# Decode attention, one core: last V slab and last wo stripe in three pieces each, and unused matmuls in the tensor engine's last waits

## Chip, cores, metric

One core of one Trainium2 chip. The metric is device time in microseconds (us) of that core, as the median of several executions. The profile is one execution; its span is about 2 us shorter than the time reported for the same execution.

## The reference

Two independent copies (A and B) of a one-token attention step. The output is A and B side by side.

```python
# B=2 batches, D=576, Hq=32 query heads, Hkv=16 key/value heads, Sk=16384, Dh=128
W = min(4096, max(256, Sk // 4))                   # 4096: only the last 4096 cache rows
q = (x @ wq)...                                    # 2 x 32 heads x 128
k, v = k_cache[:, :, Sk-W:, :], v_cache[...]       # each kv head serves two query heads
p = softmax(q @ k.T * Dh**-0.5)
o = p @ v
return o.reshape(B, 1, Hq*Dh) @ wo                 # wo: 4096 x 576
```

Everything is bf16. K and V windows of A and B are 134 MB, and each byte is used once. So this is a streaming problem.

## The kernel before

The work is cut into 32 slabs (16 kv heads of A, then 16 of B). A slab is 2 MB of K and 2 MB of V. V of a slab lies in SBUF as 64 columns j: each is a 128 x 128 tile with 128 cache rows (64 of either batch entry) on the partitions. Four slabs make a group, and a group needs a stripe of wo (8 rows per partition, 1152 KB). All loads go out on SyncE's queue in a fixed order through a ring of eight 2 MB slots. The last loads of the program are V of slab 31 and then the last stripe of wo. Both are already cut in two:

```python
v_cut = KR - 8          # 56 of 64 columns, then 8
w_cut = 7               # 7 of 8 rows, then 1
...
# issue(), wo stripe i (last one: NG - 1)
cuts = [(0, 8, wo_sem[sl])] if i < NG - 1 else [(0, w_cut, wo_sem[sl]), (w_cut, 8, wlast_sem)]
...
# issue(), last V slab: two DMAs fa (columns 0..v_cut) and fb (v_cut..KR), each with its semaphore
```

What follows the last V columns is a chain over four engines:

```python
# make_PV, last group: V columns are the weights, 16 columns of p^T move
for j in range(j0, j1):
    # ...  (col is worked out from j)
    e.matmul(OL[m % 2][:, 0:16], ring[:, r, j*128:(j+1)*128], pT[:, v, col:col+16],
             start=(j == 0), stop=(j == KR - 1))
# make_A_last (VectorE): oA = OL * cmr            - normalise and spread
# make_rl     (TensorE): 2 matmuls with jmask     - bring the heads into the layout of wo
#             (ScalarE): oP = copy of the PSUM
# make_proj   (TensorE): for each of the 8 rows j of wo, two halves of 288 output columns
for j in range(j0, j1):
    for half in range(2):
        e.matmul(PJ[half], oP[:, v, j, :], wob[:, v, j, half*NH:(half+1)*NH], ...)
# PJ[0] and PJ[1] lie on different 32-partition groups of one PSUM bank.
# make_E: VectorE copies half 0, ScalarE half 1, then SyncE issues the output store.
```

## Time and profile before

| | before |
|---|---|
| time, median of 3 | 370.21 us (370.14 to 370.30) |
| span of the profile | 368.2 us |
| DMA | 153.1 MB at 416 GB/s over the span |
| TensorE busy | 72% |
| last wo landing that TensorE waited for | 363.43 us |
| from the start of the output copies to the end of the span | 2.56 us |

From the page of the kernel before. The second to fourth lines are slices of the span, forty to a row: granted TensorE clock in tenths, DMA busy in tenths, and GB/s. The last is the share of the chain of waits by engine.

```profile
span 368.2 us, 3673 instructions
...
PEclk9966998898998779658996988895898889788755
DMA  8999999999999999999999999999999999999992
GB/s 321 448 409 431 432 427 423 433 424 425 429 424 431 429 427 421 433 431 428 424 423 433 427 427 427 424 427 429 429 423 433 429 427 421 432 429 427 425 415 97
...
DMA 81%; DVE 12%; PE 5%; issue 1%; SPq 0%; ACT 0%
```

The DMA engines are full from the first slices to the last but one. So the kernel runs at the speed of its loads, and only what comes after the last bytes can be shortened without moving fewer bytes. PEclk ends in a 5: half clock (0.50 granted in every window from 353 to 365 us).

The end of the chain of waits (start, length, what):

```profile
330.02 33.41 DMA wob<-in_B_wo_dram
363.43 0.14 issue
363.57 1.84 PE pj L670 x14
365.41 0.28 PE pj L660 x2
365.69 0.43 DVE out_sb L680
```

The timeline of the same end (start, length, engine, line, operation, operands; in brackets the idle time of the engine before it and what ended that; PE is TensorE, PEld its weight loads, DVE VectorE, ACT ScalarE, SPq the sequencer of SyncE):

```profile
360.41 1.88 PE L583 MATMUL st<-pT,ring 128*128 128x16 bf16 x64 [2.44 <-DMA ring<-in_B_v_cache_dram]
...
362.60 0.22 PE L638 MATMUL tb<-jmask,oA 128*128 128x8 bf16 x2 [0.32 <-DVE oA L618]
362.86 0.19 ACT L642 ACTIVATE oP<-tb 128x16 bf16<-128x16 f32 x1 [15.49 <-PE tb L638]
...
363.57 1.84 PE L670 MATMUL pj<-wob,oP 128*2 128x288 bf16 x14 [0.75 <-DMA wob<-in_B_wo_dram]
...
365.20 0.45 PE L660 MATMUL pj<-wob,oP 128*2 128x288 bf16 x2
...
365.72 0.40 ACT L681 ACTIVATE out_sb<-pj 2x288 bf16<-2x288 f32 x1 [2.67 <-PE pj L660]
366.59 0.32 SPq L684 DMA_DIRECT2D out_dram<-out_sb  x1
```

PV of slab 31 waits 2.44 us for V. The projection waits for wo until 363.57 and then has 14 matmuls ahead of it before it can take the last two. The store is issued 0.47 us after ScalarE's copy ended (365.72 + 0.40 = 366.12).

### The profile page before, as it was taken

The page shows a single profiled execution, that of the slowest core. Times are in us where ns is not written, and L with a number is a line of the kernel's source. Part 1 is how long each engine was busy: PE and PEld are TensorE (multiplying, and loading weights), DVE is VectorE, ACT ScalarE, POOL GpSimd, SP SyncE. Part 2 cuts the span into 40 slices and gives each one's busy share as a digit, 9 for nine tenths or more (in the row PEclk, how much of TensorE's full clock was granted, in tenths as well). Part 3 has the DMA queues.
Part 4 walks back from the last instruction along what each step waited for, and adds up shares of the span by engine and source line. Part 5 has one row for each costly group of instructions (what it writes and reads, how often), then busy time and mean ns, then how long its engine had stood idle before and what let it go on. Part 6 is the DMA issues. An engine that isn't in the chain of part 4 may idle for free.

```text
span 368.2 us, 3673 instructions
## 1 busy us (share of the span) xinstructions
PE 265.2 (72%) x1686; PEld 98.0 (27%) x1430; DVE 186.0 (51%) x189; ACT 34.3 (9%) x114; POOL 14.2 (4%) x53
## 2 busy tenths in 40 slices
PE   0635975897759499597869697777968678489754
PEld 0311111122114122242215221242313122144543
DVE  2105986967642774444843774436744476342000
ACT  1011002002000110002000110002000030003000
POOL 5010000000000000000000000000000000000000
PEclk9966998898998779658996988895898889788755
DMA  8999999999999999999999999999999999999992
GB/s 321 448 409 431 432 427 423 433 424 425 429 424 431 429 427 421 433 431 428 424 423 433 427 427 427 424 427 429 429 423 433 429 427 421 432 429 427 425 415 97
DMA packets 10976, 153.34 MB, mean 416 GB/s; under 512 B 1224, under 2 KB 1360, under 8 KB 1616
## 3 DMA queue, kind: packets, MB, share of 16 engines
q1 hardware_dynamic: 10948, 153.10, 98.0%
q8 instruction: 12, 0.20, 0.2%
q14 instruction: 4, 0.03, 0.0%
q10 hardware_dynamic: 12, 0.01, 0.0%
HBM read 153.10 MB, written 0.00 MB: 416 GB/s over the span
## 4 chain that ended last, share of the span: by engine, by line
DMA 81%; DVE 12%; PE 5%; issue 1%; SPq 0%; ACT 0%
DMA ring<-in_B_k_cache_dram 41%; DMA ring<-in_A_k_cache_dram 27%; DVE xt L426 11%; DMA wob<-in_B_wo_dram 9%; DMA ring<-in_A_wq_dram 4%; PE st L450 2%; PE st L381 1%; PE ot L274 1%; PE pj L670 1%; PE tb L607 0%; SPq L373 0%; DVE out_sb L680 0%; DVE ssum L525 0%; DVE nMrep L484 0%; PE pj L660 0%
## 5 line engine op out<-in xcount | busy, mean ns | idle before, releaser
L426 DVE STREAM_TRANSPOSE xt<-ring 128x2048 f32<-128x2048 f32 x64 | 144.4, 2287 | 88.8 <-DMA ring<-in_A_k_cache_dram 44.6
L450 PE MATMUL st<-xt,zq 128*128 128x512 bf16 x256 | 113.9, 445 | 63.6 <-DVE xt L426 63.3
L381 PE MATMUL st<-xt,zq 128*128 128x512 bf16 x256 | 114.5, 447 | 0.0
L450 PEld LDWEIGHTS st<-xt,zq 128*128 128x128 bf16 x256 | 28.0, 109 | 158.0 <-DVE xt L426 86.6
L574 PE MATMUL ot<-ring,pT 128*32 128x512 bf16 x448 | 58.7, 409 | 1.4 <-DMA ring<-in_B_v_cache_dram 0.7
L574 PEld LDWEIGHTS ot<-ring,pT 128*32 128x32 bf16 x448 | 21.4, 102 | 37.6 <-issue 18.9
L607 PEld LDWEIGHTS tb<-selv,oE 128*128 128x128 f32 x112 | 18.1, 245 | 5.7 <-issue 4.0
L413 POOL TENSOR_TENSOR zq<-qs,bmask 128x64 bf16<-128x64 bf16 x32 | 9.3, 294 | 270.0 <-PE st L381 189.9
L607 PE MATMUL tb<-selv,oE 128*128 128x16 f32 x112 | 17.0, 297 | 0.8 <-ACT oE L597 0.8
L626 DVE TENSOR_TENSOR oA<-tb,cmask 128x256 bf16<-128x256 f32 x7 | 3.0, 425 | 28.5 <-PE tb L607 28.5
L597 ACT ACTIVATE oE<-ot,rsb 128x512 f32<-128x512 f32 x14 | 9.6, 685 | 81.1 <-PE ot L574 81.1
L501 ACT ACTIVATE pR<-st,bias_sb 128x256 bf16<-128x256 f32 x32 | 15.9, 545 | 0.3
L583 PE MATMUL st<-pT,ring 128*128 128x16 bf16 x256 | 7.5, 174 | 5.8 <-DMA ring<-in_B_v_cache_dram 5.8
L670 PE MATMUL pj<-wob,oP 128*2 128x288 bf16 x126 | 10.8, 322 | 1.0 <-DMA wob<-in_B_wo_dram 0.7
L460 DVE TENSOR_REDUCE mx<-st 128x2 f32<-128x512 f32 x16 | 10.0, 664 | 1.3 <-PE tb L638 1.3
L520 DVE STREAM_TRANSPOSE pT<-pR 128x512 bf16<-128x512 bf16 x16 | 10.4, 686 | 0.0
L490 PE MATMUL tb<-ones_f,nMrep 1*128 1x1 f32 x32 | 5.6, 276 | 6.1 <-DVE nMrep L484 6.1
L494 ACT ACTIVATE bias_sb<-tb 128x2 f32<-128x2 f32 x8 | 1.4, 172 | 91.4 <-PE tb L490 91.4
L255 PE MATMUL tb<-ident_b,xt 2*128 2x2 bf16 x36 | 2.3, 194 | 10.0 <-DVE xt L222 10.0
L642 ACT ACTIVATE oP<-tb 128x16 bf16<-128x16 f32 x8 | 1.5, 191 | 84.8 <-PE tb L638 84.8
L583 PEld LDWEIGHTS st<-pT,ring 128*128 128x128 bf16 x256 | 7.1, 104 | 6.5 <-DMA ring<-in_B_v_cache_dram 6.5
L618 DVE TENSOR_TENSOR oA<-st,cmr 128x64 bf16<-128x64 f32 x4 | 0.9, 224 | 14.8 <-PE st L583 14.8
(62 smaller groups left out, 85.0 us busy)
## 6 DMA issues: line engine op xcount, KB each, us to landing
ring<-in_A_k_cache_dram SPq DMA_DIRECT2D x16, 2048.0 KB, 32.8
ring<-in_A_v_cache_dram SPq DMA_DIRECT2D x16, 2048.0 KB, 35.2
ring<-in_B_k_cache_dram SPq DMA_DIRECT2D x16, 2048.0 KB, 36.5
ring<-in_B_v_cache_dram SPq DMA_DIRECT2D x15, 2048.0 KB, 36.8
ring<-in_A_wq_dram SPq DMA_DIRECT2D x1, 4608.0 KB, 13.7
ring<-in_B_wq_dram SPq DMA_DIRECT2D x1, 4608.0 KB, 24.2
wob<-in_A_wo_dram SPq DMA_DIRECT2D x4, 1152.0 KB, 33.0
wob<-in_B_wo_dram SPq DMA_DIRECT2D x3, 1152.0 KB, 32.4
```

Source lines behind the costliest of these rows:

```text
L381: return e.add_instruction(mybir.InstMatmult(name=nc.get_next_instruction_name(), engine=mybir.EngineType.PE, ins=[e.lower_ap(mv), e.lower ...
L413: return e.tensor_tensor(dst, src, msk, ALU.mult)
L426: Xop[(t, jb)] = S.add("dve", lambda e: e.transpose(xt[:, n % NXT, :].bitcast(FP32), ring[:, r, jb * HW_:(jb + 1) * HW_].bitcast(FP32)), d ...
L450: last = e.matmul(st[bk][:, 0:512], wt, mv, start=first, stop=True, skip_group_check=True)
L460: mxs = [S.add("dve", lambda e, jb=jb: e.tensor_reduce(mx[:, jb, :], st[jb][:, :].rearrange("p (x t) -> p t x", t=2), AX.X, ALU.max), [Sop ...
L501: last = e.activation(pR[:, jb, :].rearrange("p (x t) -> p t x", t=2)[:, t, :], st[jb][:, :].rearrange("p (x t) -> p t x", t=2)[:, t, :], ...
L520: chain[(G, "pT%d" % jb)] = S.add("dve", lambda e, jb=jb: e.transpose(pT[:, v, 512 * jb:512 * jb + 512].rearrange("p (w j q) -> p j w q", ...
L574: last = e.matmul(OTB[32 * c:32 * c + 32, :], pT[:, v, col:col + 32], ring[:, r, j * 128:(j + 4) * 128], start=(j % 32 == 0), stop=(j % 32 ...
L583: last = e.matmul(OL[m % 2][:, 0:16], ring[:, r, j * 128:(j + 1) * 128], pT[:, v, col:col + 16], start=(j == 0), stop=(j == KR - 1))
L597: evac_op[(G, pr)] = S.add("act", lambda e: e.activation(oE[:, pr, :], OTB[:, :], ACTF.Copy, scale=rsb[:, v, pr:pr + 1]), deps, "oE%d_%d" ...
L607: last = e.matmul(bank[:, 0:16], oE[:, pr, 128 * c:128 * c + 128], selv[:, pr, c, :], start=(pr == 0 and c == 0), stop=(pr == 1 and c == 3))
L670: last = e.matmul(PJ[half], oP[:, v, j, :], wob[:, v, j, half * NH:(half + 1) * NH], start=(proj_start(G) and j == 0), stop=True, skip_gro ...
```

## The change

The intent: let most of the last slab's PV and of the projection run before the last bytes land, and keep TensorE busy through the waits so that its clock is full when the last work comes. The diff, cut to its core:

```diff
-        v_cut = KR - 8
-        w_cut = 7
+        v_cuts = [0, 28, 52, KR]
+        w_cuts = [0, 4, 7, 8]
...
-                cuts = ... [(0, w_cut, wo_sem[sl]), (w_cut, 8, wlast_sem)]
+                cuts = ... [(w_cuts[k], w_cuts[k + 1], ([wo_sem[sl]] + lastw_sem)[k]) for k in range(3)]
...  (V of the last slab: a loop over three DMAs in place of fa and fb)
+        def filler(n):            # n matmuls 128x128 by 512 columns; the first loads weights of ones,
+            def f(e):             # the others keep them; output into a PSUM bank that is free by then
+                wt, mv = ones_b[:, :], xt[:, 0, 0:512]
+                e.matmul(ST[(NG - 1) % 2][0][:, 0:512], wt, mv, start=True, stop=True, ...)
+                for _ in range(n - 1):
+                    last = mm_held(e, ST[(NG - 1) % 2][0][:, 0:512], wt, mv, True)
+                return last
...
                 PVop[i] = S.add("pe", f, deps, "PV%d_%d" % (i, j0))
+                if i == NSLAB - 1:
+                    filler(3 if j0 == 0 else 1)      # 3 after V piece 1, 1 after pieces 2 and 3
...
                 make_A_last(i)
+                if i == NSLAB - 3:
+                    filler(8)                        # after PV of slab 29
             if i == NSLAB - 1:
                 make_rl(NG - 1)
+                filler(1)                            # while ScalarE makes oP
```

More of the change, by code (lines that the diff above doesn't have):

```diff
@@ L150, in build_kernel @@
         ring_sem = [sem("ring%d" % r) for r in range(NR)]
-        last_sem = sem("lastv")
-        wlast_sem = sem("lastw")
+        lastv_sem = [sem("lastv%d" % k) for k in range(2)]
+        lastw_sem = [sem("lastw%d" % k) for k in range(2)]
         wq_sem = [sem("wq%d" % P) for P in range(NPROB)]
@@ L341, in issue @@
                 deps = [proj_op[i - 2]] if i >= 2 else []
-                cuts = [(0, 8, wo_sem[sl])] if i < NG - 1 else [(0, w_cut, wo_sem[sl]), (w_cut, 8, wlast_sem)]
+                cuts = [(0, 8, wo_sem[sl])] if i < NG - 1 else [
+                    (w_cuts[k], w_cuts[k + 1], ([wo_sem[sl]] + lastw_sem)[k]) for k in range(3)]
                 stream_dma[key] = []
@@ L362, in issue, with f @@
                 s0 = src_t[:, g, Sk - W:Sk, :].rearrange("b (r j) d -> r b j d", j=KR)
-                def fa(e):
-                    return e.dma_start(ring[:, r, 0:v_cut * 128], s0[:, :, 0:v_cut, :].rearrange("r b j d -> r b (j d)")).then_inc(ring_sem[r], 16)
-                def fb(e):
-                    return e.dma_start(ring[:, r, v_cut * 128:SW], s0[:, :, v_cut:KR, :].rearrange("r b j d -> r b (j d)")).then_inc(last_sem, 16)
-                stream_dma[key] = dma_op("sp", ring_sem[r], 1, fa, deps, "%s%da" % key)
-                stream_dma[("tail", 0)] = dma_op("sp", last_sem, 1, fb, deps, "%s%db" % key)
+                stream_dma[key] = []
+                for k in range(3):
+                    def f(e, c0=v_cuts[k], c1=v_cuts[k + 1], sm=([ring_sem[r]] + lastv_sem)[k]):
+                        return e.dma_start(ring[:, r, c0 * 128:c1 * 128],
+                                           s0[:, :, c0:c1, :].rearrange("r b j d -> r b (j d)")).then_inc(sm, 16)
+                    stream_dma[key].append(dma_op("sp", ([ring_sem[r]] + lastv_sem)[k], 1, f, deps, "%s%d_%d" % (key + (k,))))
                 return
@@ L385, in mm_held, with f1 @@
                 tile_size=(128, 128), tile_position=(0, 0)))
+        def filler(n):
+            def f(e):
+                wt, mv = ones_b[:, :], xt[:, 0, 0:512]
+                e.matmul(ST[(NG - 1) % 2][0][:, 0:512], wt, mv, start=True, stop=True, skip_group_check=True)
+                for _ in range(n - 1):
+                    last = mm_held(e, ST[(NG - 1) % 2][0][:, 0:512], wt, mv, True)
+                return last
+            def f1(e):
+                return e.matmul(ST[(NG - 1) % 2][0][:, 0:512], ones_b[:, :], xt[:, 0, 0:512], start=True, stop=True, skip_group_check=True)
+            S.add("pe", f1 if n == 1 else f, [exp_op[NG - 1], Xop[(NSLAB - 1, 1)]], "filler")
         Xop = {}
@@ L563, in make_PV @@
             if i == NSLAB - 1:
-                parts = [(0, v_cut, stream_dma[("V", i)]), (v_cut, KR, stream_dma[("tail", 0)])]
+                parts = [(v_cuts[k], v_cuts[k + 1], stream_dma[("V", i)][k]) for k in range(3)]
             for j0, j1, dma in parts:
```

## The prediction

> **What bounds the kernel now.** HBM traffic. The page's slice row has the DMA engines at 9 tenths in every slice but the first and last, at about 427 GB/s; the chain of waits is 81% DMA, and from 330.0 us it is one DMA of wo rows until 363.43 us. TensorE is 72% busy. Only what follows the last bytes can be shortened: span 368.2 us, so 4.8 us after that landing.
>
> **The tail before (timeline).** PV of the last slab (64 matmuls 128x16) waits 2.4 us for the V DMA and runs 360.41 to 362.29; oA 362.32, relayout matmuls 362.60, oP 362.86; 14 projection matmuls start at 363.57 with the landing and take 1.84 us; the last two end at 365.65; copies, store and end take 2.6 us more. The windows view grants clock 0.50 from 345.5 us on: a pair of projection matmuls takes 0.26 us here and 0.145 us at 328.84 us, at full clock.
>
> **What the change does.**
> 1. V arrives as 28, 24 and 12 columns instead of 56 and 8. Estimate from 29 ns per PV matmul: only 12 x 29 = 0.35 us instead of 1.9 us remain behind the last piece. But PV ends 1.1 us before the wo landing anyway, so this mostly makes room.
> 2. wo arrives as 4, 3 and 1 rows instead of 7 and 1. Today 14 matmuls (1.84 us) stand behind the first landing. Afterwards 8 can run before it.
> 3. Cost: one more piece each of V and wo. From packet durations (51 ns for 1152 B, 305 ns for 8064 B, so about 9 ns fixed, plus a 9 ns semaphore packet; 8 rows per engine and piece) about 0.08 us per piece, 0.16 us in all, on the critical path.
> 4. Fillers: 14 matmuls of 512 columns, 0.43 us each at half clock, 0.22 at full. Eight sit in a 3.0 us wait: harmless. Three and one between the V pieces, one after, one behind the relayout: at half clock these eat most of what step 1 freed.
>
> **Do the fillers raise the clock?** [...] its clock records change at multiples of 3.413 us. Cold windows filled with 512-column matmuls were followed by full clock (321.6 to 325.1 us); those with 16-column PV matmuls were not (345.5 to 352.4 us, 2.9 and 3.1 us busy). Eight fillers last one window at half clock, so they fill one only if the phase is lucky; the later ones fill some 60%. I expect full clock in the projection in less than half of the runs.
>
> **Sum.** Cold: last projection matmul at about 365.2 instead of 365.65, gain 0.2 to 0.4 us. Warm: projection keeps up with the landings; it ends at the last landing (363.43 + 0.5 for the last piece's own + 0.16) plus 0.4 us, about 364.5: gain 1.1 us. Weighted: about 0.7 us, 0.2%.
>
> Predicted time 369.5 us, range 368.9 to 370.2. Chances: faster by over 2% 0.01, within 2% 0.98, slower 0.01.
>
> **What would show it.** Right: last wo landing within 0.3 us of 363.9; the first 8 projection matmuls start before it; fewer than 4 stand behind it. Granted clock above 0.5 in the last 8 us shows step 4 works. Wrong: first projection matmul not before 363.5, or TensorE continuously busy from 359 to 365 at 0.50 (fillers on the critical path).
>
> **What would make it wrong.** Small pieces slowing the DMA more; an instruction fetch colliding with one DMA engine at the end (one 16 KB fetch took 1.1 us at 361.0); fillers delaying the last PV.

"Its clock records" are those of the trace of before: the clock changes there only in whole steps of 3.41 us (half from 331.88, full from 335.29, half again from 345.53 us), and a window is one such step. That a window has to be filled for the clock to rise was the estimate from the windows named there.

## The result, and the profile after

| | before | after |
|---|---|---|
| time, median of 6 | 370.25 us (369.96 to 370.58) | 368.46 us (368.31 to 368.85) |
| ratio | | 0.9952 (95%: 0.994 to 0.9965) |
| span of the profile | 368.2 us | 366.6 us |

A ratio is the mean time of one kernel's runs over that of the other's from the same rounds, so it is not quite the ratio of the medians. Gains quoted below for the runs are differences of those same means. Here it is 1.76 us, or 0.5%. The result is faster than the predicted range (368.9 to 370.2), and more than twice the predicted gain of 0.7 us.

The answering lines of the page after:

```profile
span 366.6 us, 3694 instructions
...
PEclk9976897698985889895895998867798989958958
DMA  8999999999999999999999999999999999999994
...
DMA 82%; DVE 13%; PE 4%; SPq 0%; issue 0%
```

The DMA engines are as full as before, and PEclk now ends in an 8. The end of the chain:

```profile
324.29 36.06 DMA ring<-in_B_v_cache_dram
...
360.39 0.81 PE st L594 x24
361.20 0.44 PE st L395
361.64 0.31 PE st L594 x12
361.95 0.44 PE st L395
362.39 0.09 PE tb L651 x2
362.48 0.45 PE st L395
362.93 1.38 PE pj L683 x14
364.31 0.17 PE pj L673 x2
364.48 0.43 DVE out_sb L693
```

The chain no longer ends in the wo load. It leaves the DMA at the landing of the second V piece (360.35), and TensorE then works without a gap until 364.48. Three fillers (line 395, 0.44 us each) are part of that chain. The timeline:

```profile
362.27 0.21 PE L651 MATMUL tb<-jmask,oA 128*128 128x8 bf16 x2
...
362.52 0.19 ACT L655 ACTIVATE oP<-tb 128x16 bf16<-128x16 f32 x1 [14.45 <-PE tb L651]
...
362.86 1.45 PE L683 MATMUL pj<-wob,oP 128*2 128x288 bf16 x14
363.75 0.23 PEld L683 LDWEIGHTS pj<-wob,oP 128*2 128x2 bf16 x6 [0.33 <-DMA wob<-in_B_wo_dram]
...
364.14 0.29 PE L673 MATMUL pj<-wob,oP 128*2 128x288 bf16 x2
...
364.50 0.40 ACT L694 ACTIVATE out_sb<-pj 2x288 bf16<-2x288 f32 x1 [1.79 <-PE pj L673]
364.99 0.31 SPq L697 DMA_DIRECT2D out_dram<-out_sb  x1
```

The projection starts at 362.86 instead of 363.57. It takes 1.61 us until the copies start at 364.47, where it took 2.11 us before (363.57 to 365.68). Then the kernel needs 2.09 us to its end (366.56 − 364.47) where it needed 2.56 (368.24 − 365.68). These three terms, 0.71, 0.50 and 0.47, are the whole difference of the two spans (1.68 us). The first is the pieces. The second should be the clock, and the windows agree (stretch, length, busy (count), granted clock, DMA share, GB/s), first before, then after:

```profile
core 0: us, PE busy (x), PEclk, DMA share, GB/s
359.00:362.00 3.00, 1.59 (x59) 0.50 0.66 264
362.00:363.50 1.50, 0.50 (x13) 0.50 0.19 67
363.50:365.00 1.50, 1.43 (x14) 0.50 0.00 0
```

```profile
359.00:362.00 3.00, 2.63 (x56) 0.73 0.76 297
362.00:363.50 1.50, 1.50 (x10) 0.50 0.24 85
363.50:365.00 1.50, 0.93 (x13) 0.91 0.01 2
```

Most of the third term is in the timeline's last line: the store is issued 0.09 us after ScalarE's copy ended (364.90), not 0.47. The other 0.09 us lie behind the store's issue (1.57 us to the end of the span, 1.65 before). Nothing in the diff touches the copies or the store.

### The profile page after: what moved, and what is told of

Its sections match the earlier page's. It is cut to its first block, busy times and chain, and to the rows that moved or that the text cites. A ratio compares the mean times of both kernels' runs of the same rounds, so it can differ in the third digit from the quotient of the medians.

```text
span 366.6 us, 3694 instructions
## 1 busy us (share of the span) xinstructions
PE 271.8 (74%) x1700; PEld 101.0 (28%) x1435; DVE 185.9 (51%) x189; ACT 34.3 (9%) x114; POOL 14.1 (4%) x53
## 4 chain that ended last, share of the span: by engine, by line
DMA 82%; DVE 13%; PE 4%; SPq 0%; issue 0%
DMA ring<-in_B_k_cache_dram 41%; DMA ring<-in_A_k_cache_dram 28%; DVE xt L437 12%; DMA ring<-in_B_v_cache_dram 10%; DMA ring<-in_A_wq_dram 4%; PE ot L274 1%; PE st L461 1%; PE st L381 1%; PE pj L683 0%; PE st L395 0%; SPq L373 0%; PE st L594 0%; SPq L368 0%; DVE out_sb L693 0%; DVE ssum L536 0%
## 5 line engine op out<-in xcount | busy, mean ns | idle before, releaser
L461 PE MATMUL st<-xt,zq 128*128 128x512 bf16 x256 | 115.6, 452 | 62.6 <-DVE xt L437 62.5
L381 PE MATMUL st<-xt,zq 128*128 128x512 bf16 x256 | 115.6, 451 | 0.0
L585 PE MATMUL ot<-ring,pT 128*32 128x512 bf16 x448 | 55.1, 395 | 0.7 <-ACT oE L610 0.7
L585 PEld LDWEIGHTS ot<-ring,pT 128*32 128x32 bf16 x448 | 20.5, 100 | 33.8 <-issue 15.4
L620 PEld LDWEIGHTS tb<-selv,oE 128*128 128x128 f32 x112 | 21.1, 280 | 5.8 <-issue 4.0
L620 PE MATMUL tb<-selv,oE 128*128 128x16 f32 x112 | 19.8, 324 | 0.8 <-ACT oE L610 0.8
```

What stands on the lines that cost most here:

```text
L381: return e.add_instruction(mybir.InstMatmult(name=nc.get_next_instruction_name(), engine=mybir.EngineType.PE, ins=[e.lower_ap(mv), e.lower ...
L461: last = e.matmul(st[bk][:, 0:512], wt, mv, start=first, stop=True, skip_group_check=True)
L585: last = e.matmul(OTB[32 * c:32 * c + 32, :], pT[:, v, col:col + 32], ring[:, r, j * 128:(j + 4) * 128], start=(j % 32 == 0), stop=(j % 32 ...
L620: last = e.matmul(bank[:, 0:16], oE[:, pr, 128 * c:128 * c + 128], selv[:, pr, c, :], start=(pr == 0 and c == 0), stop=(pr == 1 and c == 3))
```

## The experiments

Theory 1 after this reading: the pieces let the projection start earlier; the fillers raise the clock in it, if the grid of times on which the clock changes (356.94, 360.36 and 363.77 us in after, 3.41 us apart) happens to fit; and the store's 0.4 us is something else. Rival 2 is that the pieces do everything. Rival 3 is that the fillers do everything. Each kernel gave correct results and was timed in five rounds beside the kernel before.

| run | edit | median (range), us | gain of means, us |
|---|---|---|---|
| e1 | pieces, no fillers | 368.97 (368.71 to 369.06) | 1.38 |
| e2 | fillers, two pieces | 369.33 (369.17 to 370.23) | 0.68 |
| e3 | wo in three, V in two, no fillers | 369.27 (369.19 to 369.44) | 1.02 |
| e4 | the changed kernel again | 368.64 (368.23 to 369.12) | 1.64 |
| e5 | before + one SyncE instruction | 369.75 (369.67 to 370.02) | 0.46 |
| e6 | changed kernel, early fillers only | 368.88 (368.72 to 369.00) | 1.41 |
| e7 | pieces, no fillers, projection in quarters | 368.54 (368.38 to 368.67) | 1.75 |
| e8 | e2 + one SyncE instruction | 369.64 (369.55 to 369.85) | 0.62 |
| e9 | e7 with V in two pieces | 368.56 (368.43 to 368.75) | 1.67 |
| e10 | changed kernel, more fillers | 368.33 (368.09 to 369.39) | 1.63 |
| e11 | changed kernel + quarters | 368.64 (368.37 to 368.74) | 1.64 |
| e12 | changed kernel, late fillers only | 368.51 (368.23 to 368.85) | 1.80 |

e1 to e4 ran on one chip and share the runs of before; so do e5 to e8, and e9 to e11; e12 ran alone.

### e1: the pieces without the fillers

```diff
-                if i == NSLAB - 1:
-                    filler(3 if j0 == 0 else 1)
-                if i == NSLAB - 3:
-                    filler(8)
-                filler(1)
```

> The change without its fillers: three pieces of V and of wo, no unused matmul. Theory 1 (pieces and a raised clock both count): granted clock 0.50 from about 346 us to the end, the last projection matmul about 0.4 us later after the last slab's middle V landing than in the changed kernel, time about 368.9 us, gain of 1.3 us on before. Rival 2 (the pieces do everything, the clock does not matter): same time as the changed kernel, 368.4 to 368.5 us. Rival 3 (the fillers do everything): about 370.2 us.

Measured: 368.97 us, a gain of 1.38 us. The projection in e1's timeline:

```profile
362.74 1.87 PE L681 MATMUL pj<-wob,oP 128*2 128x288 bf16 x14 [0.43 <-DMA wob<-in_B_wo_dram]
...
364.89 0.45 DVE L691 CAST out_sb<-pj 2x288 bf16<-2x288 f32 x1 [2.85 <-PE pj L671]
```

It starts at 362.74 because the first wo piece lands then, and at half clock takes 2.15 us (to 364.89). Most of the gain is there without any filler, and the fillers add something (e4, same rounds: 0.26 us more). The runs of e1 and e4 overlap, so this pair alone does not settle it; but the sixteen runs with the late fillers (after, e4, e12) gain 1.74 us on average and the ten without (e1, e6) 1.39, a difference of 0.34 us (95%: 0.19 to 0.49), across different rounds. Rival 3 falls. Rival 2 is nearly right but not quite.

### e2: the fillers with two pieces

The cuts are set to 56 and 8 columns, and 7 and 1 rows. The eight fillers stay after slab 29; five stand ahead of the last slab's PV, one after its second piece and one after the relayout.

```diff
+        v_cuts = [0, 56, KR]
+        w_cuts = [0, 7, 8]
...  (loops over two pieces in place of three)
+            if i == NSLAB - 1:
+                filler(5)
-                    filler(3 if j0 == 0 else 1)
+                if i == NSLAB - 1 and j0 > 0:
+                    filler(1)
```

> The fillers without the pieces: V and wo arrive in two pieces as before; the fillers stand in the same waits, cut to fit: eight after the last slab but two, five ahead of the last slab's PV, one behind it, one behind the relayout. Theory 1: if the clock is full from about 361 us, the sixteen projection matmuls take 1.2 us instead of 2.1, gain up to 0.9 us, time about 369.3 to 369.8; if it stays half, no gain or a loss of up to 0.3 us. Rival 2 (clock does not matter): 370.2 or more. Rival 3 (the fillers do everything): about 368.5.

Measured: two modes, 370.19 and 370.23, and 369.17 to 369.33. The trace fell in the slow mode. Its clock records show full clock from 355.51 to 362.34 us and half clock from there on, so the projection just missed it: it ran from 363.60 to 365.71, 2.11 us, as before. That the fast mode is full clock in the projection fits its size of 1.0 us, but no trace of that mode was taken.

### e3: wo alone in three pieces

```diff
-        v_cuts = [0, 28, 52, KR]
+        v_cuts = [0, 56, KR]
...  (and no fillers, as in e1)
```

> wo in three pieces, V in two as before, no fillers. Theory 1: PV of the last slab ends at about 362.1 to 362.4 us as before, projection starts at about 363.0 us and not with the last landing; at half clock it is 2.1 us of work, so it ends at about 365.1: gain 0.5 us, time about 369.7. If the third V piece is worth nothing, the time equals that of the pieces without fillers.

Measured: 369.27 us. The projection starts at 362.99, right behind oP, and ends at 365.11, as expected. The time is 0.4 us better than expected, and that is again the store: 0.10 us behind ScalarE's copy. The third V piece is worth e1 against e3, 0.36 us.

### e4: the changed kernel again

> The changed kernel unaltered, for its spread and a second trace. Theory 1 expects 368.3 to 368.9 us, and the grid on which the clock changes at another place in time, [...]. The 0.46 us between the last copy and the issue of the output store, seen in the trace of before and 0.07 us in the trace of the changed kernel, is expected to be chance: it should take either value in these four traces.

Measured: 368.64 us, 368.23 to 369.12. In this trace the clock rose only at 364.84 (363.77 in after, so the grid lies 1.07 us later), after the projection, which took 2.11 us (362.62 to 364.73). So the same program runs with the projection at half or partly at full clock. One expectation was wrong: the gap ahead of the store is not chance. It was short in all of e1, e3 and e4, and long only in e2 and before.

### e5: one more instruction on SyncE

What before and e2 share is two pieces of wo and so fewer SyncE instructions. In their traces the store is SyncE's 80th recorded instruction (79 ahead of it); in after, e1, e3 and e4 it has 80 or 81 ahead of it. The test is the kernel before with one instruction more: a wait on the load of x, which landed long before.

```diff
-                deps = [proj_op[i - 2]] if i >= 2 else []
+                deps = ([proj_op[i - 2]] if i >= 2 else []) + ([x_dma] if i == NG - 1 else [])
```

> The kernel before with one more instruction on SyncE and nothing else: a wait for a load that landed long ago, ahead of the last wo loads. In the four traces whose wo comes in three pieces, SyncE issues the output store 0.06 to 0.08 us after its wait for ScalarE's copy ends; in the two whose wo comes in two (before, and the fillers with two pieces) 0.44 us after. Theory A (it is the place of the store in SyncE's instruction stream, which one more instruction shifts): the gap falls to 0.08 us and the time to about 369.85 us, gain 0.37. Theory B (it comes with the loads themselves): the gap stays 0.44 us, time 370.2.

Measured: 369.75 us, a gain of 0.46 us where 0.37 was expected. The interval of the ratio (0.9988, 0.9975 to 1.0) just reaches 1, but the five runs (369.67 to 370.02) and the nine of before beside them (370.03 to 370.40) do not overlap. Copy and store in e5's timeline:

```profile
365.65 0.40 ACT L681 ACTIVATE out_sb<-pj 2x288 bf16<-2x288 f32 x1 [2.70 <-PE pj L660]
366.15 0.32 SPq L684 DMA_DIRECT2D out_dram<-out_sb  x1
```

The projection is where it was (363.50 to 365.62), and the store is issued 0.10 us behind the copy (366.05). Between the end of SyncE's wait and the store the traces of before and e2 have 0.43 us, all twelve others, this one included, 0.05 to 0.06. Theory A holds: a quarter of the gain of the change is the place of one instruction in SyncE's stream.

The traces show more. In eight of them (after, e1, e4, e6, e7, e10, e11, e12) a gap of 0.42 us stands between two wo issues that otherwise follow each other within 0.05 us. In after (SyncE's timeline, windows 333:335 and 335.5:341):

```profile
333.73 1.71 SPq L347 DMA_DIRECT2D wob<-in_B_wo_dram  x2
335.86 3.86 SPq L347 DMA_DIRECT2D wob<-in_B_wo_dram  x1
```

The first two end at 335.44. In all ten traces with a visible gap it lies behind SyncE's 79th recorded instruction. In the other four (e3, e5, e8, e9) the 79th is the last wo issue, and SyncE then waits about 30 us or more for the copies anyway. So the cost has not gone: it stays at one place of the stream, and an instruction more moves the output store to the far side of that place. And in all 14 traces a DMA on the instruction queue q14 follows the place: 1.0 us behind it in before and e2 (367.20 us in before), 3.6 to 4.2 us behind it in the twelve others.

What happens there is not shown. No run counts the instructions up to the place, and none shows whether the DMA on q14 has to do with the gap.

### e6: early fillers only

```diff
-                    filler(3 if j0 == 0 else 1)
+                if i == NSLAB - 1 and j0 == 0:
+                    filler(3)
-                filler(1)
```

> The changed kernel without its three single fillers (behind the second and third V piece and behind the relayout); the eight and the three stay. Theory 1 [...]: the clock is up at about 356 to 360 us but half again in the projection, time as without any filler, 368.9 us (368.7 to 369.1). Theory 2 (the single fillers only delay the last slab): 368.2 us or less. Theory 3 (the eight do the work): as the changed kernel, 368.5.

Measured: 368.88 us, the value of e1. In the trace the clock was full from 356.68 to 360.10 and half in the projection. So the eight and the three raise the clock where it is of no use.

### e7: the projection in four quarters

If the clock matters only because 2 us of projection lie behind the landings, there should be another way to shorten it. The two halves, whose outputs lie on different 32-partition groups, already seem to run side by side: a pair takes 0.233 us in before (363.57 to 365.20 over seven rows, half clock), and one alone would take about 0.25 us (an estimate from the fillers of after, 512 columns in 0.44 us at half clock). That four would do the same was not shown before this run. So the output is cut into four times 144 columns:

```diff
-        PJ = [PJB[32 * i:32 * i + Bb, 0:NH] for i in range(2)]
+        NQ = NOUT // 4
+        PJ = [PJB[32 * i:32 * i + Bb, 0:NQ] for i in range(4)]
...  (matmuls and copies loop over four quarters; VectorE copies two, ScalarE two; no fillers)
```

> Three pieces, no fillers, and the projection cut in four column quarters of 144 [...] in place of two halves of 288. If the clock matters only because the projection's 16 matmuls are on the critical path (theory 1), halving that work at half clock (estimate: 1.05 us in place of 2.1) gains about as much as the raised clock does: the last matmul at about 364.1 to 364.3 us, copies 0.15 us longer, time 368.2 to 368.5 us in every run, with a smaller spread than the changed kernel. If the landings bind instead, no gain over the pieces alone, 368.97.

Measured: 368.54 us, 368.38 to 368.67. This is the changed kernel's time without a single filler, and it holds less spread. The timeline:

```profile
362.60 0.65 PE L683 MATMUL pj<-wob,oP 128*2 128x144 bf16 x16 [0.46 <-DMA wob<-in_B_wo_dram]
...
363.59 0.53 PE L683 MATMUL pj<-wob,oP 128*2 128x144 bf16 x12 [0.34 <-DMA wob<-in_B_wo_dram]
...
363.94 0.29 PE L673 MATMUL pj<-wob,oP 128*2 128x144 bf16 x4
```

The first rows' matmuls are done in 0.65 us, and TensorE then waits for wo (0.34 us in the bracket). The clock was 0.50 throughout. The landings bind now, not the engine. This supports the reading that the clock mattered only through the length of the projection. And the four quarters do run side by side: in e9, where 28 of these matmuls run back to back, a row of wo takes 0.114 us (362.99 to 363.79 over seven rows), half of the 0.233 us before.

### e8: e2 with the SyncE instruction

> The fillers with two pieces, plus the same extra SyncE instruction. Theory A: both modes of that kernel (370.2 and 369.2 us) move down by 0.37 us, to 369.85 and 368.85. Theory 1 on the two modes: they are the projection at half and at full clock, 1.0 us apart; the trace of one run tells which: at half clock the 16 projection matmuls take 2.1 us, at full 1.2.

Measured: one mode only, 369.55 to 369.85. Against the slow mode of e2 (370.2, other rounds) it is about 0.55 us faster, and its gap ahead of the store is the short one, so theory A holds here too. The second part is inconclusive: none of the five runs fell in a fast mode, and the trace has the projection at half clock (it dropped at 362.64).

### e9: quarters, V in two pieces

> The projection in four column quarters, no fillers, wo in three pieces, V in two as before. With the quarters the projection waits for the wo landings (first at about 362.6, second 363.55, last 363.9 us), so theory 1 says that the third V piece, which lets it start at 362.6 in place of 363.0, is no longer needed: PV ends at about 362.2, the first eight rows' worth ends before 363.6, time 368.4 to 368.6 us, the same as quarters with three V pieces within 0.15 us. If the third V piece still matters, about 368.85.

Measured: 368.56 us, the same as e7. The projection starts 0.4 us later (362.99), and its last four matmuls start at 363.79, only 0.14 us after the last landing (363.65). The third V piece had only bought an earlier start for a projection that was too slow.

### e10: more fillers

```diff
-                    filler(3 if j0 == 0 else 1)
+                    filler(5 if j0 == 0 else 1)
-                    filler(8)
+                    filler(14)
-                filler(1)
+                filler(3)
```

> The changed kernel with more fillers: fourteen, five, one, one and three, in place of eight, three, one, one and one. If the spread of the changed kernel (368.2 to 369.1 us) is the clock's phase, and the clock in the projection is worth up to 0.8 us, filling longer makes full clock there likelier: the trace shows it full through the projection, 368.1 to 368.3 us in most runs. Where it stays half, the extra fillers delay the projection: 369.3 or more. If fillers only help by their present number, all runs are slower than the changed kernel.

Measured: three runs at 368.09 to 368.33, two at 369.10 and 369.39. The two modes are there, but the slow one is not what was expected. Its trace, and its windows:

```profile
353.34 5.16 PE L381 MATMUL st<-xt,ones_b 128*128 128x512 bf16 x13
...
358.33 2.47 PE L594 MATMUL st<-pT,ring 128*128 128x16 bf16 x92
...
364.12 1.02 PE L683 MATMUL pj<-wob,oP 128*2 128x288 bf16 x14
...
365.30 0.45 DVE L693 CAST out_sb<-pj 2x288 bf16<-2x288 f32 x1 [2.04 <-PE pj L673]
```

```profile
356.00:359.00 3.00, 3.00 (x35) 0.71 1.00 404
...
363.50:365.00 1.50, 1.50 (x20) 1.00 0.00 0
```

The clock was full in the projection, which took 1.18 us (364.12 to 365.30): against 2.11 us this is the direct measure of the clock's worth, 0.93 us. But the clock had risen late (357.76 us), the fourteen fillers ran mostly at half speed, slab 30's PV started at 358.33 instead of about 356, and everything behind it came late. A filler that is late on its own costs what it was to win.

### e11: quarters and fillers together

> The changed kernel, fillers included, with the projection in four column quarters. Theory 1: the raised clock and the quarters shorten the same 2 us of projection, so together they gain no more than the quarters alone (368.54 us): 368.4 to 368.7, bound by the last wo landing. Rival (the clock helps elsewhere too): 368.1 or less.

Measured: 368.64 us, no more than the quarters alone. Clock and quarters shorten the same stretch; they do not add. The one trace has the clock at half in the projection (it dropped at 360.06) and shows TensorE waiting 0.27 us for wo there, so full clock and quarters together were not seen.

### e12: late fillers only

```diff
-                if i == NSLAB - 3:
-                    filler(8)
```

> The changed kernel without its eight early fillers; the three and the three single ones stay. In the trace of the changed kernel the clock that was full at the end of the projection came after a cold window of three late fillers and the first projection matmuls, and the raised clock from the eight had ended by 360.4 us. If that is so (theory 1), the eight are not needed: 368.4 to 368.7 us as the changed kernel, below the 368.9 us without late fillers. If the eight prepare the raise, 368.9 or, as the three now run at half clock before the second V piece, up to 369.1.

Measured: 368.51 us, a gain of 1.80 us, the same as the changed kernel. In its trace the clock was half until 363.69 and full from there, as in the changed kernel's trace, and the projection took 1.62 us (362.75 to 364.37). So the eight early fillers do nothing measurable for the time.

## Why the prediction was wrong, point by point

Two steps of it failed: the 2.6 us behind the projection, which it took as fixed, and the cost of the fillers at half clock. Both made the predicted gain too small.

- **Bound by its loads, and only the tail to win: right.** No run gained more than 2.3 us. (Whether HBM or the DMA engines set the rate, no run tells.)
- **The cost of the extra pieces, 0.16 us: right.** From the last packet of the last whole slab to the last packet of wo, the four traces with two pieces each (before, e2, e5, e8) take 7.74 us, the two with three pieces of wo (e3, e9) 7.79 to 7.81, the others 7.85 to 7.90. So, on average, the piece of wo costs 0.06 us, that of V 0.09, and both 0.15.
- **Where the projection starts: roughly right.** The signs named were met: the last wo landing within 0.3 us of 363.9 (364.07), the first eight matmuls before it, and two behind it. But its sign for "wrong", TensorE busy without a gap and fillers on the critical path, was nearly met too (360.39 to 364.48, three fillers in the chain), and the kernel was faster all the same.
- **"copies, store and end take 2.6 us more": this step failed.** It was carried into both sums as a constant. From the start of the copies it measured 2.56 us before and 2.09 us after the change. The runs put the loss of 0.47 us at one place of SyncE's stream, and one more SyncE instruction ahead of it takes it off the critical path (e5: 0.46 us). A reader of the first profile could have seen the 0.47 us between ScalarE's copy and the store in the timeline, an idle step with nothing to wait for, and asked what would move it.
- **"at half clock these eat most of what step 1 freed": this failed too.** Measured from the last packet of the last whole slab, the relayout comes after 7.01 us before, 6.99 in e3, 6.39 in e1 and 6.49 after (6.60 in e4). The third V piece freed 0.6 us, and the fillers took back 0.1 to 0.2. They mostly run while TensorE waits for V or for VectorE and ScalarE anyway, and in e1 the projection waits for the first wo piece even so.
- **The cold sum, "at about 365.2": mis-sized.** With the projection at half clock it measured 364.73 in e4 and 364.89 in e1, so 0.8 to 0.95 us earlier than before's 365.68 rather than 0.2 to 0.4. The prediction's own reason for the small gain was the fillers, and they cost far less.
- **The warm sum, 364.5: right, in part by luck.** It measured 364.47 and 364.37 in the two traces with a raised clock at the end of the projection, and there the last two matmuls start within 0.15 us of the last landing, as the sum has it. But the clock was full only from 363.77 and 363.69 on, a phase that the sum did not assume.
- **Clock raised in "less than half of the runs": not settled.** Of the three traces with the late fillers of the change (after, e4, e12) two had full clock for the end of the projection and none for all of it; e11, with the same fillers and the projection in quarters, had half. The spread of 368.2 to 369.1 us fits a matter of phase, but times alone do not tell the modes apart. The runs of e2 and e10 show that one program has two modes.

The gain adds up, as differences of means from the runs: 0.46 us for the SyncE instruction (e5), 0.56 for the third wo piece (e3 less e5, different rounds, so an estimate), 0.36 for the third V piece (e1 less e3), and 0.26 for the fillers (e4 less e1). The sum is 1.64 us for e4; the first measurement of the changed kernel gave 1.76.

No version clearly beats the changed kernel. The quarters (e7, e9) equal it with no unused work and no dependence on the clock's phase.

## What to carry to other kernels

When a stream of loads ends, cut the last load so that only a sliver of work stands behind it; a piece cost 0.06 to 0.09 us here and the third piece of wo won about 0.56. A full clock bought with unused matmuls is a matter of phase (the same program had it at the end of the projection in after, not in e4) and helped only where 2 us of real work stood behind the landings; making that work shorter with four quarters of the output side by side in place of two halves (0.114 us for a row of wo in place of 0.233) gave the same, every time. And read every idle step of the tail: a constant that nobody questions, here the store's 0.43 us, can be as large as the effect one is studying.

## What the traces show of the clock, the gap and a piece, and what they leave open

- In the traces of before and after the clock changes on a grid of 3.41 us, and the full stretches of e2 (355.51 to 362.34 us, 6.83) and e6 (356.68 to 360.10, 3.42) fit it. Which matmuls raise it is not shown. Before the change TensorE was busy for 2.90 us of the window from 345.53 us and 3.07 us of the next, mostly with 16-column PV matmuls and with projection matmuls whose weights have 2 columns, and the clock stayed at half. The share of busy time alone does not explain it: after the change TensorE was busy for all 3.41 us of the window from 350.12 us, with the same kinds of matmul and 0.3 us of the first filler, and the clock stayed at half, while full clock followed the next window (also 3.41 us, mostly fillers) and the one from 360.36 us (3.38 us, with three whole fillers). In all six traces in which the eight 512-column fillers ran (after, e2, e4, e6, e8, e11) the clock rose during or just behind them (at 356.94 us in after, 355.51 in e2); in e1 and e7, without any filler, it was 0.50 from 353 to 365 us.
- The gap at one place of SyncE's stream was 0.43 us in front of the output store before the change and came off the critical path with one more instruction. What causes it, and how to find its place before a run, is not shown.
- One piece more inside a full queue cost 0.06 us for wo and 0.09 us for V. The time from the last data packet to the landing was 0.49 us for the first piece of the last wo stripe before the change (362.94 to 363.43), so little of it shows in the cost of a piece.
